# Opening of a retention and two-layer kernel: first half tile of weights loaded second, keys scaled in their own step

## The chip, the cores and the metric

One core of one Trainium2 chip. The metric is the device time of one execution in microseconds (us), as the median of several runs.

## What is computed

Four sequences of 576 tokens, 8 heads of 64 columns, go through a retention layer (attention whose scores are multiplied by a decay in place of a softmax), then through two pairs of dense layers, one with a softplus and one with a sigmoid gate between them:

```python
gamma = 1.0 - 2.0 ** (-5.0 - np.arange(H))
Dmat = np.where(rel >= 0, gamma[:, None, None] ** rel[None, :, :], 0.0)   # rel = i - j
x = ((q @ k.T / 8) * Dmat) @ v            # per batch and head, then 2304 tokens x 512
h = x @ w_in;   x = softplus(h) @ w_out   # w_in 512 x 2048, w_out 2048 x 512
h = x @ w_in2;  out = (h * sigmoid(1.702 * h)) @ w_out2
```

## The kernel before, in words

Every engine has its own queue and works it off in order; the order in which the program issues instructions is the order of these queues, and the framework adds the waits between engines.

**First batch.** `first_batch` (L568) computes the retention of batch 0 before anything else can start. Its work is eight "pairs" i = 0 to 7: two heads by 256 tokens each, of which odd i are the later tokens of the heads of i-1. The loop at L607 runs ten times; iteration i calls `step(i - 2, i, ...)` (L387), which puts the scores and the state sums of pair i and the output of pair i-2 through TensorE (PE). In the order of PE's queue, step i is: scores k by q (L409); for odd i a small product of the last 64 tokens; the state sums, scaled keys by values (L397, `ps<-w_kqv`); then the output of pair i-2 from the known state (`<-w_kqv,w_sv`) and from its masked scores (`<-w_a,w_kqv`). Then ScalarE (ACT) multiplies the scores with the decay of the rows (L436, twice) and, for even i, copies the state sums (L94, `w_sv<-ps_h`); VectorE (DVE) updates the state (L443, called state update below), for odd i masks the last scores (L450), and writes the output xf (L456, and L461 for odd i); GpSimd (POOL) masks the scores (L446). The sums of state and the output of one step lie in one bank of PSUM.

**Scaling of keys.** Before the state sums, the keys of each pair are multiplied with a decay by `scale_pair` (L373): one head on ACT (L385) and one on POOL (L383); for pair 0 both on ACT. `scale_pair(i + 1, "ap", "p")` at L614 issues POOL's half of pair i+1 ahead of step i, `scale_pair(i + 2, "ap", "a")` at L619 ACT's half of pair i+2 behind step i.

**Split for the first layer.** PE multiplies in parts: every operand is split into a rounded high part and the rest. Behind each odd step from 3 on, `split_x` issues ACT's cast xh of two pairs (L94) and, one iteration later, DVE's subtraction xl (L99). One quarter of xh and xl belongs to each pair of heads; the last quarter comes in two halves behind iterations 8 and 9. The first layer (`run_first`, `mm1`, L220; its matmuls are at L211) starts when the loop is over, and needs the four quarters one after the other.

**Weights.** Each weight arrives as a 64-bit word and is turned into high and low part by `convert_first` (L113), a generator of which `next` issues a piece. For one half tile (a unit): `get`, ACT's rescaling (L132); `go`, DVE's L104 and L105; `merge`, DVE's L110; ACT's cast (L94, `w<-wa`); DVE's subtraction (L99, `w<-wa,w`). Units 0 and 1 are the first layer's weights of the first two of 16 blocks, unit 2 those of the third, unit 3 the first of the second layer's. How many pieces follow each iteration stands in the table at L689.

**Loads.** SyncE (SP) issues the loads of the eight pairs (512 KB each), of the decays, of the last tokens ("ends"), and of the weights (512 KB each) in the order of L586 to L602. SP's queue issues a transfer when the eighth before it has landed: while loads are pending, its issue times are landing times.

Of the kernel before, what the change touches and what calls it, by code (L numbers as in the profile page):

```python
# [33 lines left out]
def kernel(  # L34
# [37 lines left out]
    B, _, NPAIR, _, KQV = kqv.shape  # L72
# [19 lines left out]
    def hi(eng, dst, src):  # L92
        if eng == "a":
            nc.scalar.copy(dst, src)  # L94
        else:
            nc.vector.tensor_copy(dst, src)
# [5 lines left out]
    def shift(w, a):  # L102
        u = a.bitcast(U32)
        nc.vector.tensor_single_scalar(out=u, in_=u, scalar=3, op=ALU.logical_shift_left)  # L104
        nc.vector.scalar_tensor_tensor(  # L105
            out=u, in0=w[:, :, 1], scalar=0x80000000, in1=u, op0=ALU.bitwise_and, op1=ALU.bitwise_or)

    def merge(w, a):
        u = a.bitcast(U32)
        nc.vector.scalar_tensor_tensor(  # L110
            out=u, in0=w[:, :, 0], scalar=29, in1=u, op0=ALU.logical_shift_right, op1=ALU.bitwise_or)

    def convert_first(units, slots, raw, tiles, loaded, made):  # L113

        opening, n = 3, len(units)
        held, shifted, room = {}, set(), {}  # L120

        def words(i):
            k, m = units[i][0], len(units[i])
            return raw[k // 2][:, k % 2:k % 2 + m].rearrange("p s n two -> p (s n) two")

        def get(i):
            if i < n and i not in held and all(k in loaded for k in units[i]):
                k, m = units[i][0], len(units[i])
                if k // 2 not in room:
                    room[k // 2] = wr.tile([P, 2, DM], F32, tag="wa", name="wa")  # L130
                a = room[k // 2][:, k % 2:k % 2 + m].rearrange("p s n -> p (s n)")
                nc.scalar.mul(a, words(i)[:, :, 1].bitcast(F32), 2.0 ** -112)  # L132
                held[i] = a

        def go(i):
            shift(words(i), held[i])
            shifted.add(i)

        for i in range(n):
            while i not in held:  # L140
                get(i)
                yield
            if i not in shifted:
                go(i)
                if 0 < i < opening:
                    get(i + 1)
                yield
            merge(words(i), held[i])
            yield
            if i >= opening:  # L150
                get(i + 1)
            k, m = units[i][0], len(units[i])
            if k // 2 not in tiles:
                tiles[k // 2] = wp.tile([P, 2, 2, DM], F32R, tag="w", name="w")
            h, l = (tiles[k // 2][:, k % 2:k % 2 + m, j] for j in range(2))
            a = held[i].rearrange("p (s n) -> p s n", s=m)
            hi("a", h, a)
            if i >= opening and i + 2 < n and len(units[min(i + 1, n - 1)]) == 1:
                get(i + 2)
            yield  # L160
            if i >= opening and i + 1 in held and (m == 2) == (len(units[i - 1]) == 2):
                go(i + 1)
                yield
            lo(l, a, h)
            made.update(slots[k] for k in units[i])
            if i < opening:
                get(i + 1) if i == 0 else None
            yield

    def convert(n, ready, words, place, begin, end):  # L170
# [133 lines left out]
    with tc.manual_schedule():  # L304
# [36 lines left out]
        with ExitStack() as consts, ExitStack() as right, ExitStack() as second:  # L341
            ac = consts.enter_context(tc.tile_pool(name="ac", bufs=1))
            ap = right.enter_context(tc.tile_pool(name="ap", bufs=2, side="right"))
# [29 lines left out]
            def scale_pair(i, engines="aa", only="ap"):  # L373
                p, x = pairs[i][2], loaded[i][2]
                if i >= 2 * NPAIR:
                    nc.scalar.mul(x, x, sdec64[:, p:p + 1])
                    return
                for h in range(2):
                    y, d = x[:, :, halves[h]], sdec[:, 2 * p + h:2 * p + h + 1]
                    if engines[h] not in only:  # L380
                        continue
                    if engines[h] == "p":
                        nc.gpsimd.tensor_scalar(out=y, in0=y, scalar1=d, scalar2=None, op0=ALU.mult)  # L383
                    else:
                        nc.scalar.mul(y, y, d)  # L385
# [182 lines left out]
            def first_batch():  # L568

                n = 2 * NPAIR  # L570
                xf[0] = xf_tile()
                raw = [wp.tile([P, 2, KQV], F32, tag="w", name="w_kqv") for _ in range(NPAIR)]
                end = wp.tile([P, 2, KQV], F32, tag="w", name="w_end")
                end = end.rearrange("p s n -> p (s n)")[:, 0:NPAIR * ENDS].rearrange("p (a n) -> p a n", a=NPAIR)
                sv0 = wp.tile([P, 2, 8, P], F32, tag="w", name="w_sv")
                sv0 = [[sv0[:, i, j, 0:D] for j in range(4)] for i in range(2)]
                a0 = wp.tile([P, 4 * DM], F32, tag="w", name="w_a")
                a0 = [a0[:, i * (2 * C0 + D):(i + 1) * (2 * C0 + D)] for i in range(3)]

                def load(i):  # L580
                    load_pair(i, raw[i // 2][:, i % 2], end[:, i // 2])

                def load_end(p, n):
                    nc.sync.dma_start(out=end[:, p:p + n], in_=ends[0, :, p:p + n])

                load(0)  # L586
                nc.sync.dma_start(out=dec, in_=decays)
                load(1)
                load_end(0, 1)
                load(2)  # L590
                w1_load(0)
                load(3)
                nc.sync.dma_start(out=odec, in_=outdecay)
                load_end(1, 1)
                load(4)
                w1_load(1)
                load(5)
                load_end(2, 2)
                load(6)
                w1_load(2)  # L600
                load(7)
                w1_load(3, 4, 5)  # L602
                scale_pair(0)
                scale_pair(1, "ap", "a")
                yield
                late = []
                for i in range(n + 2):  # L607
                    if i % 2:
                        banks = [bank(ps_y, "y") for _ in range(3)]
                    else:  # L610
                        so = ps_a.tile([P, 2, T], F32, tag="so", name="ps_so")
                        banks = [bank(ps_h, "h"), so[:, 0], so[:, 1]]
                    if i + 1 < n:
                        scale_pair(i + 1, "ap", "p")  # L614
                    while late:
                        late.pop(0)()
                    step(i - 2 if i >= 2 else None, i if i < n else None, banks, sv0, a0)
                    if i + 2 < n:
                        scale_pair(i + 2, "ap", "a")  # L619
                    if i == n:  # L620
                        late.append(split_x(0, 1, xf[0], NPAIR - 1, slice(0, C0)))
                    elif i == n + 1:
                        late.append(split_x(0, 1, xf[0], NPAIR - 1, slice(C0, T)))
                    elif i >= 3 and i % 2:
                        late.append(split_x(0, 1, xf[0], i // 2 - 1))
                    for _ in range(1 if i < FILL else 0):
                        warm()
                    if i == n + 1:
                        while late:
                            late.pop(0)()  # L630
                    yield
# [29 lines left out]
            def w1_load(*ks):  # L661

                for k in ks:
                    if k >= len(slots):
                        continue
                    if k // 2 not in w1_raw:
                        w1_raw[k // 2] = wp.tile([P, 2, DM, 2], U32, tag="w", name="w_raw")
                    f, s = slots[k]
                    nc.sync.dma_start(
                        out=w1_raw[k // 2][:, k % 2].rearrange("p n two -> p (n two)"),  # L670
                        in_=w_src(w1_in, w1_out, f, s))
                    w1_loaded.add(k)
# [12 lines left out]
            for i, _ in enumerate(first_batch()):  # L685
                if i == 9:
                    w1_load(6, 7)
                    nc.sync.dma_start(out=dmask.rearrange("p a d -> p (a d)"), in_=masks)
                for _ in range({5: 2, 7: 2, 8: 2, 9: 2}.get(i, 1) if i >= 2 else 0):  # L689
                    next(w1_gen, None)  # L690


# [696 lines left out]
```

## Time and profile before

| what | value |
|---|---|
| time before, median of 3 runs | 837.8 us (835.58, 837.8, 838.04) |
| the profiled execution's own time | 835.43 us |
| its span, first to last instruction | 833.7 us |
| PE busy | 822.2 us, 99% of the span |
| DVE, ACT, POOL busy | 583.7, 407.6, 99.6 us |
| granted clock of PE, mean | 0.999 of full speed |

A row of the timeline gives the start of an instruction from the span's start, its duration, the engine, the line, the operation, output <- inputs, how many instructions are merged (x2), and in brackets how long the engine stood idle before it and what ended that. The next start on the same engine can lie before the end of an instruction, since they overlap a little in the engine.

### The profile page before, as it was taken

To read this page: it belongs to the slowest core of one execution; us is meant where nothing else is said; L and a number is where in the kernel's file an instruction comes from. 1 tells how busy PE (TensorE), PEld (TensorE's weight loads), DVE (VectorE), ACT (ScalarE), POOL (GpSimd) and SP (SyncE) were. 2 spreads that over 40 slices of the span, in tenths; PEclk is the share of its full clock that TensorE was granted. 3 is DMA by queue.
4 is the path that set the end of the run, shared out by engine and by line. 5 is a ranking of instruction groups with operands and counts; after the bars stand their busy time and mean duration, and the time that the engine had idled before them with its cause. 6 is when DMAs were issued, how large, how long until landed. Compare 5 with 4: busy or idle time off the path is not lost.

```text
span 833.7 us, 17016 instructions
## 1 busy us (share of the span) xinstructions
PE 822.2 (99%) x6810; PEld 742.0 (89%) x6811; DVE 583.7 (70%) x1206; ACT 407.6 (49%) x797; POOL 99.6 (12%) x185
## 2 busy tenths in 40 slices
PE   8899999999999999999999999999999999999998
PEld 6788788888888888998888899999999999999997
DVE  3999996666676664775543667787778777866665
ACT  5666654433443434453434545554555555554332
POOL 3200001111211120001011011211121111111010
PEclk9999999999999999999999999999999999999999
DMA  9966325887787674899996677887799778776691
GB/s 339 407 272 244 119 88 188 274 270 239 236 262 263 231 236 171 303 359 387 418 367 210 227 279 243 314 316 241 260 328 320 242 266 327 280 246 215 234 361 55
DMA packets 63438, 221.71 MB, mean 266 GB/s; under 512 B 6448, under 2 KB 20080, under 8 KB 50304
## 3 DMA queue, kind: packets, MB, share of 16 engines
q0 software_dynamic: 21600, 122.76, 42.4%
q1 hardware_dynamic: 41440, 97.62, 32.1%
q8 instruction: 53, 0.87, 0.4%
q10 hardware_dynamic: 320, 0.26, 0.1%
q14 instruction: 25, 0.20, 0.1%
HBM read 163.99 MB, written 56.62 MB: 265 GB/s over the span
## 4 chain that ended last, share of the span: by engine, by line
PE 79%; issue 8%; DVE 7%; DMA 3%; ACT 1%; POOL 1%; SPq 0%; POOLq 0%; ACTq 0%
PE y L211 22%; PE ph L211 22%; PE ph L893 17%; PE m L893 16%; PE ps_so L477 3%; DMA xo<-x 1%; DMA w_kqv<-kqv 1%; POOL w L812 1%; DVE wa L110 1%; DVE wa L105 1%; DMA w_end<-ends 1%; DVE wa L104 1%; DVE w L99 0%; DVE ga L99 0%; DVE sv L529 0%
## 5 line engine op out<-in xcount | busy, mean ns | idle before, releaser
L211 PE MATMUL ph<-xh,w 128*128 128x512 f32 (+1 forms) x640 | 183.4, 371 | 0.9 <-ACT xh L94 0.6
L211 PE MATMUL y<-gh,w 128*128 128x512 f32 x512 | 169.9, 392 | 0.0
L893 PE MATMUL m<-w,ga 128*128 128x256 f32 x936 | 139.5, 282 | 0.1
L211 PEld LDWEIGHTS ph<-xh,w 128*128 128x128 f32 x640 | 114.8, 188 | 22.5 <-ACT xh L94 1.0
L893 PEld LDWEIGHTS m<-w,ga 128*128 128x128 f32 x936 | 124.0, 190 | 0.3 <-DVE ga L99 0.3
L211 PE MATMUL ph<-xl,w 128*128 128x512 f32 (+1 forms) x320 | 117.9, 368 | 0.0
L211 PEld LDWEIGHTS y<-gh,w 128*128 128x128 f32 x512 | 95.9, 188 | 20.1
L893 PE MATMUL ph<-xo_c,w 128*128 128x256 f32 x768 | 108.2, 283 | 0.8 <-DVE he L1140 0.8
L893 PE MATMUL ph<-xo,w 128*128 128x256 f32 x768 | 105.8, 283 | 1.4 <-DVE ho L1180 0.8
L893 PEld LDWEIGHTS ph<-xo,w 128*128 128x128 f32 x768 | 97.7, 189 | 3.0 <-DVE ho L1180 1.9
L893 PEld LDWEIGHTS ph<-xo_c,w 128*128 128x128 f32 x768 | 97.8, 188 | 2.2 <-DVE he L1140 1.4
L211 PE MATMUL y<-gl,w 128*128 128x512 f32 x256 | 99.8, 390 | 0.0
L265 ACT ACTIVATE g<-ph 128x512 f32<-128x512 f32 (+1 forms) x80 | 44.1, 552 | 96.4 <-PE ph L211 90.7
L893 PE MATMUL m<-w,gb 128*128 128x256 f32 x576 | 89.7, 282 | 0.0
L99 DVE TENSOR_TENSOR gl<-g,gh 128x512 fp32r<-128x512 f32 x64 | 44.0, 688 | 54.9 <-ACT gh L94 54.6
L893 PEld LDWEIGHTS m<-w,gb 128*128 128x128 f32 x576 | 78.0, 191 | 0.0
L211 PEld LDWEIGHTS ph<-xl,w 128*128 128x128 f32 x320 | 60.2, 188 | 10.2 <-DVE xl L99 0.2
L99 DVE TENSOR_TENSOR gb<-g,gb 128x256 fp32r<-128x256 f32 x112 | 43.9, 420 | 24.8 <-ACT gb L94 24.7
L94 ACT CAST ga<-g 128x512 fp32r<-128x512 f32 x80 | 49.6, 621 | 15.9 <-DVE g L745 6.5
L211 PEld LDWEIGHTS y<-gl,w 128*128 128x128 f32 x256 | 48.1, 188 | 9.5
L99 DVE TENSOR_TENSOR ga<-g,ga 128x512 fp32r<-128x512 f32 x80 | 52.6, 685 | 0.4 <-ACT ga L94 0.2
L104 DVE TENSOR_SCALAR wa<-wa 128x512 uint32<-128x512 uint32 (+1 forms) x53 | 25.9, 488 | 32.3 <-ACT wa L179 32.3
(147 smaller groups left out, 1119.0 us busy)
## 6 DMA issues: line engine op xcount, KB each, us to landing
w<-sums_out POOLq DMA_DIRECT2D x40, 1024.0 KB, 7.9
w<-sums_in POOLq DMA_DIRECT2D x32, 1024.0 KB, 5.3
raw<-kqv SPq DMA_DIRECT2D x24, 512.0 KB, 5.3
w<-kept POOLq DMA_DIRECT2D x12, 1024.0 KB, 8.9
w_raw<-w_in SPq DMA_DIRECT2D x16, 512.0 KB, 9.3
w_raw<-w_out SPq DMA_DIRECT2D x16, 512.0 KB, 9.9
raw<-w_in POOLq DMA_DIRECT2D x16, 512.0 KB, 5.8
raw<-w_out POOLq DMA_DIRECT2D x16, 512.0 KB, 5.7
```

The source lines that it names most:

```text
L94: nc.scalar.copy(dst, src)
L99: nc.vector.tensor_tensor(out=dst, in0=src, in1=f32(h), op=ALU.subtract)
L104: nc.vector.tensor_single_scalar(out=u, in_=u, scalar=3, op=ALU.logical_shift_left)
L105: nc.vector.scalar_tensor_tensor(out=u, in0=w[:, :, 1], scalar=0x80000000, in1=u, op0=ALU.bitwise_and, op1=ALU.bitwise_or)
L110: nc.vector.scalar_tensor_tensor(out=u, in0=w[:, :, 0], scalar=29, in1=u, op0=ALU.logical_shift_right, op1=ALU.bitwise_or)
L211: nc.tensor.matmul(out_ap, l, r, start=first and i == 0, stop=last and i == k - 1)
L265: nc.scalar.activation(g, ph, AF.Softplus)
L477: nc.tensor.matmul(z[halves[m], o, at:at + D], l[halves[g]], rhs[halves[g]], start=clear[o][m], stop=True, skip_group_check=True)
L812: nc.gpsimd.dma_start(out=where[i], in_=src)
L893: nc.tensor.matmul(out_ap, l, r, start=clear, stop=True, skip_group_check=True)
```

## The change

The first half tile of weights is loaded right behind pair 0 and the decays, and the second ahead of pair 4; the conversion starts behind iteration 0 and gets another number of pieces per iteration (table at L689); the rescaling `get` of units 1 and 2 is issued at another piece; and both halves of the keys' scaling of pair i are issued at the head of iteration i.

```diff
@@ convert_first
             if i not in shifted:
                 go(i)
-                if 0 < i < opening:
+                if i == opening - 1:
                     get(i + 1)
                 yield
...
             made.update(slots[k] for k in units[i])
-            if i < opening:
-                get(i + 1) if i == 0 else None
             yield
@@ first_batch
                 load(0)
                 nc.sync.dma_start(out=dec, in_=decays)
+                w1_load(0)
                 load(1)
                 load_end(0, 1)
                 load(2)
-                w1_load(0)
                 load(3)
+                load_end(1, 1)
                 nc.sync.dma_start(out=odec, in_=outdecay)
-                load_end(1, 1)
+                w1_load(1)
                 load(4)
-                w1_load(1)
                 load(5)
...
                 scale_pair(0)
-                scale_pair(1, "ap", "a")
                 yield
...
-                    if i + 1 < n:
-                        scale_pair(i + 1, "ap", "p")
+                    if 0 < i < n:
+                        scale_pair(i, "ap")
                     while late:
                         late.pop(0)()
                     step(i - 2 if i >= 2 else None, i if i < n else None, banks, sv0, a0)
-                    if i + 2 < n:
-                        scale_pair(i + 2, "ap", "a")
@@ behind the loop's iterations
-                for _ in range({5: 2, 7: 2, 8: 2, 9: 2}.get(i, 1) if i >= 2 else 0):
+                for _ in range({2: 2, 3: 2, 7: 3, 10: 2}.get(i, 1) if i else 0):
                     next(w1_gen, None)
```

Lines behind L145 move up by up to five: the scaling on ACT is L385 before and L383 in the change, the scores' decay L436 and L434, the state update L443 and L441, the output xf L456 and L454.

**ACT, steps 3 to 5, before.** The scores of pair 3 (L436), then the scaling of pair 5 (L385), the cast xh of the first quarter, step 4, the scaling of pair 6, the conversion's cast and rescaling, and the scores of pair 5:

```order
L436 ACTIVATE w_a<-ps_y,dec 128x256 x2
L385 ACTIVATE w_kqv<-w_kqv,dec 128x2x64
L94 CAST xh<-xf 128x512
L436 ACTIVATE w_a<-ps_so,dec 128x256 x2
L94 COPY w_sv<-ps_h 128x64
L385 ACTIVATE w_kqv<-w_kqv,dec 128x2x64
L94 CAST w<-wa 128x512
L132 ACTIVATE wa<-w_raw 128x512
L436 ACTIVATE w_a<-ps_y,dec 128x256 x2
```

The same place in the change, from the scores of pair 3 to those of pair 5:

```order
L434 ACTIVATE w_a<-ps_y,dec 128x256 x2
L94 CAST xh<-xf 128x512
L132 ACTIVATE wa<-w_raw 128x512
L383 ACTIVATE w_kqv<-w_kqv,dec 128x2x64
L434 ACTIVATE w_a<-ps_so,dec 128x256 x2
L94 COPY w_sv<-ps_h 128x64
L383 ACTIVATE w_kqv<-w_kqv,dec 128x2x64
L434 ACTIVATE w_a<-ps_y,dec 128x256 x2
```

The two scalings here are those of pairs 4 and 5, each directly ahead of the scores of its own pair; the cast xh and the rescaling of unit 1 stand ahead of the first.

**ACT, steps 6 and 7, in the change**, from the cast xh behind step 5 to the scores of pair 7:

```order
L94 CAST xh<-xf 128x512
L383 ACTIVATE w_kqv<-w_kqv,dec 128x2x64
L434 ACTIVATE w_a<-ps_so,dec 128x256 x2
L94 COPY w_sv<-ps_h 128x64
L94 CAST w<-wa 128x512
L132 ACTIVATE wa<-w_raw 128x512
L383 ACTIVATE w_kqv<-w_kqv,dec 128x2x64
L434 ACTIVATE w_a<-ps_y,dec 128x256 x2
```

Before, the scaling of pair 7 stood ahead of this xh and the rescaling of unit 2 ahead of the scores of pair 6; now the copy of step 6, the cast of unit 1 and the rescaling of unit 2 stand ahead of the scaling of pair 7.

**DVE, steps 6 and 7, before**, with the waits that each instruction carries (numbers aside, the names are engines and DMA queues): the state update and xf of step 6, unit 1's L110, the state update, end mask and xf of step 7, and the last subtraction of unit 1:

```order
L443 SCALAR_TENSOR_TENSOR w_sv<-w_sv,dec,ps_h 128x64 [waits Activation_49]
L456 TENSOR_TENSOR xf<-ps_h,odec 128x256
L110 SCALAR_TENSOR_TENSOR wa<-w_raw,wa 128x512 [waits DVE_49]
L443 SCALAR_TENSOR_TENSOR w_sv<-w_sv,dec,ps_y 128x64 [waits DVE_49,PE_49]
L443 SCALAR_TENSOR_TENSOR w_sv<-w_sv,dec,ps_y 128x64 [waits DVE_49]
L450 SCALAR_TENSOR_TENSOR w_a<-ps_y,dec,mask 128x64
L456 TENSOR_TENSOR xf<-ps_y,odec 128x256
L461 TENSOR_TENSOR xt<-ps_y,odec 128x64
L99 TENSOR_TENSOR w<-wa,w 128x512 [waits Activation_49]
```

The same place in the change:

```order
L441 SCALAR_TENSOR_TENSOR w_sv<-w_sv,dec,ps_h 128x64 [waits Activation_49]
L454 TENSOR_TENSOR xf<-ps_h,odec 128x256
L99 TENSOR_TENSOR w<-wa,w 128x512 [waits Activation_49]
L441 SCALAR_TENSOR_TENSOR w_sv<-w_sv,dec,ps_y 128x64 [waits DVE_49,PE_49]
L441 SCALAR_TENSOR_TENSOR w_sv<-w_sv,dec,ps_y 128x64 [waits DVE_49]
L448 SCALAR_TENSOR_TENSOR w_a<-ps_y,dec,mask 128x64
L454 TENSOR_TENSOR xf<-ps_y,odec 128x256
L459 TENSOR_TENSOR xt<-ps_y,odec 128x64
```

Unit 1's L110 has gone further up and its L99 has moved from behind step 7's group to ahead of it. In both, the row that writes xf from the out matmuls carries no wait of its own for PE; the state update ahead of it does (odd steps), or ACT's copy that it waits for (even steps).

## Rows read from the trace of the kernel before

**Rows 1.** Stretches: span, busy time (instructions) by engine, granted clock, DMA share, GB/s.

```profile
25.00:30.00 5.00, 3.84 (x40) 3.16 (x41) 4.93 (x13) 2.91 (x7) 2.49 (x4) 1.00 1.03 403
30.00:35.00 5.00, 4.39 (x19) 3.22 (x19) 4.56 (x11) 3.86 (x8) 0.00 (x0) 1.00 1.03 412
35.00:80.00 45.00, 45.00 (x403) 37.14 (x403) 43.19 (x72) 29.16 (x43) 0.00 (x0) 1.00 0.75 286
...
400.00:800.00 400.00, 397.82 (x3071) 385.13 (x3070) 278.92 (x579) 199.16 (x426) 49.39 (x93) 1.00 0.78 279
```

**Rows 2.** Timeline of ACT: scalings of pairs 1, 4, 5 and 7.

```profile
7.06 0.40 ACT L385 ACTIVATE w_kqv<-w_kqv,dec 128x128 f32<-128x128 f32 x1 [1.67 <-DMA w_kqv<-kqv]
...
13.70 0.40 ACT L385 ACTIVATE w_kqv<-w_kqv,dec 128x128 f32<-128x128 f32 x1 [0.59 <-DMA w_kqv<-kqv]
...
16.28 0.40 ACT L385 ACTIVATE w_kqv<-w_kqv,dec 128x128 f32<-128x128 f32 x1 [1.45 <-DMA w_kqv<-kqv]
...
21.52 0.40 ACT L385 ACTIVATE w_kqv<-w_kqv,dec 128x128 f32<-128x128 f32 x1 [0.34 <-DMA w_kqv<-kqv]
```

**Rows 3.** Timeline of PE: step 2, and step 5 from its state sums on.

```profile
8.87 0.71 PE L409 MATMUL ps_so<-w_kqv 64*128 64x128 f32 x8 [0.23 <-DMA w_kqv<-kqv]
9.52 0.47 PE L397 MATMUL ps_h<-w_kqv 128*64 128x64 f32 x8
...
10.28 0.66 PE L397 MATMUL ps_h<-w_a,w_kqv 128*64 128x128 f32 x8
...
17.33 0.43 PE L397 MATMUL ps_y<-w_kqv 128*64 128x64 f32 x8
...
18.87 0.28 PE L397 MATMUL ps_y<-w_a,w_end 128*64 128x64 f32 x4
```

**Rows 4.** Timeline of POOL: scaling of half of pair 2, mask of pair 1.

```profile
8.88 0.60 POOL L383 TENSOR_SCALAR w_kqv<-w_kqv,dec 128x128 f32<-128x128 f32 x1
...
9.96 0.64 POOL L446 TENSOR_SCALAR_AFFINE_SELECT w_a<-w_a 128x512 f32<-128x512 f32 x1 [0.47 <-ACT w_a L436]
```

**Rows 5.** Timeline of ACT: cast xh, rescaling, scores and copy of step 6, cast, scores of step 7.

```profile
21.83 0.60 ACT L94 CAST xh<-xf 128x512 fp32r<-128x512 f32 x1
...
22.34 0.69 ACT L132 ACTIVATE wa<-w_raw 128x512 f32<-128x512 f32 x1
...
22.92 0.83 ACT L436 ACTIVATE w_a<-ps_so,dec 128x256 f32<-128x256 f32 x2
...
23.64 0.21 ACT L94 COPY w_sv<-ps_h 128x64 f32<-128x64 f32 x1
...
25.13 0.62 ACT L94 CAST w<-wa 128x512 fp32r<-128x512 f32 x1 [1.28 <-DVE wa L110]
...
25.65 0.83 ACT L436 ACTIVATE w_a<-ps_y,dec 128x256 f32<-128x256 f32 x2
```

**Rows 6.** Timeline from pair 7's state update to the first layer's last quarter.

```profile
25.01 0.59 DVE L443 SCALAR_TENSOR_TENSOR w_sv<-w_sv,dec,ps_y 128x64 f32<-128x64 f32 x2
...
25.71 0.41 DVE L456 TENSOR_TENSOR xf<-ps_y,odec 128x256 f32<-128x256 f32 x1
...
26.18 0.68 DVE L99 TENSOR_TENSOR w<-wa,w 128x512 fp32r<-128x512 f32 x1
...
26.77 0.86 DVE L104 TENSOR_SCALAR wa<-wa 128x512 uint32<-128x512 uint32 x1
...
27.41 0.66 PE L397 MATMUL ps_y<-w_a,w_kqv 128*64 128x128 f32 x8 [1.16 <-POOL w_a L446]
27.67 0.69 DVE L105 SCALAR_TENSOR_TENSOR wa<-w_raw,wa 128x512 uint32<-128x512 uint32 x1
...
28.11 0.73 PE L211 MATMUL ph<-xh,w 128*128 128x512 f32 x2
...
30.60 0.40 ACT L94 CAST xh<-xf 128x256 fp32r<-128x256 f32 x1
31.05 0.73 PE L211 MATMUL ph<-xh,w 128*128 128x512 f32 x2 [0.61 <-ACT xh L94]
```

## The prediction

> **What bounds the kernel now.** I read the stretch table first, to see which engine each stage waits on. From 35 us to 80 TensorE (PE) is busy for 45.00 of 45.00 us, and from 400 to 800 for 397.82 of 400.00; only before 35 us does it stand still for a whole microsecond and more (3.84 of 5.00 at 25 to 30, 4.39 at 30 to 35) [rows 1]. So PE sets the time, and an edit of the opening is worth exactly what it moves one instant: the first matmul of the first layer on the last quarter of the tokens, at 31.05 us, which waits 0.61 for ScalarE's (ACT's) xh [rows 6]. Behind it PE does not stop until 80, so a later start is not made up, and VectorE (DVE), busy for 43.19 of those 45 us [rows 1], has nothing to spare for an earlier one either.
>
> I then followed that instant backwards in the timeline. Two clocks run through the opening. One is the landing of the head pairs: pair 1 at 7.06, pair 4 at 13.70, pair 5 at 16.28, pair 7 at 21.52, read from the scalings that waited for them [rows 2]; 5.24 us for the two steps from pair 5 to pair 7, one 512 KB transfer each 1.29 (13.70 to 16.28 holds two). The other is each step's chain over the engines. Today the keys of pair i+2 are scaled at the end of step i on ACT and those of i+1 at the start of step i on GpSimd (POOL), so PE finds them scaled soon after landing and the steps keep the pace of the landings. Behind the last landing the tail is a DVE queue: the state update of pair 7 starts at 25.01 and 6.04 us later, at 31.05, PE has its input [rows 6].
>
> **The change, part by part.**
>
> *Loads.* The first half tile of weights goes ahead of pair 1, so pairs 1 and 2 land one transfer later, 1.29; pair 4 too, since the second half tile goes ahead of it. Pairs 3, 5, 6 and 7 keep their place: pair 7 is the sixteenth issue of SyncE's queue both before and after. The last landing stays at 21.52, so this edit alone costs 0 to 1.3 and is swallowed by what follows. The two small transfers that swap places (decays of the output, ends of pair 1) are needed only after pair 3 has landed: nothing.
>
> *Conversion.* The same DVE operations for half tiles 0 and 1 are queued earlier; from the first operation of half tile 2 on, DVE's queue is the same row for row. The only one that leaves the tail is the last operation of half tile 1 (L99, 26.18 to 26.77, 0.59) [rows 6]; before, it lay between pair 7's state update and the end. Gain in the tail 0.6, and up to 1.0 if L104 behind it, which took 0.90 beside POOL's mask (26.77 to 27.67), no longer meets one; I take 0.8: 5.2 from pair 7's state update to PE's input.
>
> *Scaling.* This decides. ACT is one in-order queue, and the scaling of pair i now stands in it behind everything that step i-1 left there: its copy of the state sums, and its casts. PE's queue is in order as well: the state matmuls of step i wait for the scaling, and the out matmuls of pair i-2 stand behind them. So a loop closes that was open. The rows of waits show what makes it long: L454, which reads the out matmuls, carries no wait for PE, so L441 ahead of it must already have waited for all matmuls of that bank, the out matmuls included; for even steps the same goes for ACT's copy. I take these waits as they stand. No row of the trace can show them bind, as DVE and ACT were always later; the other bound is rival 2. The Trainium skill, "PSUM — Partial Sum Buffer", section "PSUM bank collisions raise a hardware error", says that two engines must not touch one bank in the same partitions at once and that schedulers therefore order such pairs; by it the sum below stands, without it rival 2 does, and no row of this trace decides.
>
> The loop from the end of an odd step's out matmuls to the next one's:
> - 0.1 handover; DVE state update, end mask and xf 1.11 (25.01 to 26.12); ACT cast xh 0.51 (21.83 to 22.34); scaling 0.40 and handover 0.05; PE state, state-out and out matmuls of the even step 1.42 (9.52 to 10.94); ACT copy 0.21 and handover; then the scaling of the odd pair 0.45; PE of the odd step from its state matmuls to its last 1.82 (17.33 to 19.15) [rows 2, 3, 5, 6]. Together 6.1.
> - From step 3 to 5, L132 of half tile 1 stands between cast and scaling, 0.58 (22.34 to 22.92): 6.7. From step 5 to 7, the cast of half tile 1, 0.52 (25.13 to 25.65), and L132 of half tile 2, 0.58, stand ahead of the scaling of pair 7 [rows 5]: 7.2.
>
> Against 5.24 for two steps of landings, so from step 3 on the landings no longer matter. Start of the count: pair 1 lands at 8.35 (7.06 + 1.29); scores 0.71, ACT's two scalings of them 0.83, POOL's mask 0.64 and, behind it in POOL's queue now, the scaling of half of pair 2, 0.60, with handovers 11.3; step 2 on PE 1.42, copy 0.2, the cast of half tile 0 that now stands there 0.52, scaling of pair 3 0.45: 13.9; step 3 on PE 1.82, handover 0.1: state update of pair 3 at 15.8 [rows 2 to 5]. Pair 5's follows at 22.5, pair 7's at 29.7; it was at 25.01. Plus 5.2: PE's input is ready at 34.9 to 35.2 in place of 31.05. **Sum: +3.9 to +4.2; I take +4.1 us.** The gaps of PE that show it: about 2.2 ahead of step 4's state matmuls, 1.6 ahead of step 6's, 1.2 ahead of step 7's; the wait of 1.16 for POOL's mask at 27.41 [rows 6] goes.
>
> The profiled execution took 835.43, which gives 839.5; the median of the runs is 837.8, which gives 841.9. Two of the four times shown stand near 835.5 and two near 837.9, so I count from their mean, 836.7: **841 us**, +0.5%. A measurement of this kernel tells about 0.3%, 2.5 us, from no change.
>
> **Rivals.**
> 1. *The forecast*, the loop through ACT's queue: 839.5 to 842. For it: each wait of the loop stands in the order rows, and each duration in a row. Against it: the sum of some fifteen handovers that I could only estimate. Chance 0.57.
> 2. *The loop is shorter*, because reads of a bank do not wait for the out matmuls. Then state update and end mask (0.70) leave the path in the three odd steps, 2.1, and the copy of an even step leaves 0.95 earlier, of which 0.2 stays in step 2, nothing in step 4 (POOL's mask and scaling, 0.64 + 0.60, take its place) and 0.8 in step 6: 3.1 less, so +1.0: 837.7. Against it: L454's missing wait. Chance 0.18.
> 3. *No effect*: the tail behind the last landing sets the end, and it only swaps one DVE operation for another delay: 836 to 837.5. For it: 21.52 stays. It needs the steps to catch up with the landings, so a loop under 5.24. Chance 0.09.
> 4. *Faster*: the casts no longer wait in ACT behind a landing, pair 7's mask comes early, and the tail loses its stalls. The most that this can give: from 21.6, scores and end 0.8, state and out matmuls of steps 7 to 9 some 4.1, then the nine matmuls of the first three quarters, 2.3 (28.11 to 30.44, where the wait of 0.61 begins) [rows 6], reach 28.8, which is 2.2 before 31.05: 834.5. It decides only if each loop stays under 5.24. Chance 0.06.
> 5. *Clock*. The granted clock is 1.00 in every stretch of the opening [rows 1], with PE gaps of 1.2 at most; the forecast's gaps are up to 2.2, three in a row. If it fell to 1.2 GHz for these steps, the PE parts of the loops, 2 x (1.42 + 1.82) and 3.2 ahead of them, would double: up to +9.7 more, 844 to 851. The Trainium skill, "TensorE: Matmul & The Clock Gate", section "A second HAM failure mode: psum-queue depth-cycling", tells of a PE that idles briefly and often between groups and swings between the two levels; by that rule this would happen here, while the trace, which has such gaps at 1.00, so far bears the opposite out. Chance 0.10.
>
> **How the numbers follow.** Slower by over 0.3%: 0.50 of case 1, all of 5 and 0.02 of 2, 0.62 in all. Within 0.3%: 0.07 of 1, 0.16 of 2, 0.08 of 3 and 0.02 of 4, so 0.33. Faster by over 0.3%: the rest of 3 and 4, 0.05. The range reaches from case 2 counted from the fast executions (835.5 + 1.0, 836.5) to case 1 counted from the slow ones with handovers 0.2 longer at a dozen places (837.9 + 4.1 + 2.4, 844.4); below lie case 4 and half of 3, above most of 5, together under 0.2.
>
> **What would show it.** Right: the scalings (now L383) start long after their landing, pair 7's near 27.5 in place of 21.52; PE waits for ACT ahead of the state matmuls of steps 4, 6 and 7; pair 7's state update near 30; first matmul of the last quarter near 35; from there the same distances as before. Wrong: scalings of pairs 5 to 7 still released by a DMA (3 or 4), state updates that start before the out matmuls of their step have ended (2), a granted clock below 1.00 before 35 us (5), or PE standing still less after 35 us than before.

## The result, and the profile after

| what | before | change |
|---|---|---|
| median, 6 runs each | 836.24 us (835.45 to 838.04) | 843.93 us (840.45 to 847.29) |
| ratio | 1 | 1.0086, 95% interval 1.0056 to 1.0115 |
| the profiled execution: own time, span | 835.43, 833.7 us | 844.08, 842.3 us |
| its granted clock, mean | 0.999 | 0.994 |

The change costs 7.7 us. First the stretches of the changed kernel, with the columns of [rows 1]: span, busy time (instructions) of PE, PE's weight loads, DVE, ACT and POOL, granted clock, DMA share, GB/s.

```profile
5.00:10.00 5.00, 2.14 (x20) 1.61 (x21) 0.28 (x1) 2.29 (x7) 0.87 (x2) 0.91 0.96 353
10.00:15.00 5.00, 5.00 (x45) 3.55 (x45) 2.48 (x6) 1.98 (x6) 2.48 (x5) 0.50 1.03 413
15.00:20.00 5.00, 3.95 (x60) 3.13 (x57) 2.42 (x8) 1.96 (x6) 1.78 (x3) 0.90 1.03 407
20.00:25.00 5.00, 3.56 (x42) 2.81 (x44) 2.34 (x6) 3.46 (x9) 1.22 (x2) 0.78 1.02 409
25.00:30.00 5.00, 3.46 (x48) 2.85 (x48) 2.46 (x7) 1.65 (x4) 1.37 (x3) 0.88 1.03 406
30.00:35.00 5.00, 4.22 (x66) 3.24 (x64) 2.13 (x7) 2.31 (x6) 3.12 (x6) 1.00 1.03 407
...
400.00:800.00 400.00, 397.80 (x3038) 383.80 (x3037) 275.29 (x573) 199.35 (x427) 47.59 (x90) 1.00 0.79 284
```

The kernel before in the same stretches, up to where [rows 1] begin:

```profile
5.00:10.00 5.00, 4.77 (x57) 3.55 (x58) 1.04 (x4) 2.76 (x9) 1.87 (x4) 1.00 0.98 358
10.00:15.00 5.00, 4.12 (x64) 3.39 (x65) 1.82 (x5) 2.92 (x8) 2.67 (x5) 1.00 1.03 412
15.00:20.00 5.00, 4.94 (x84) 3.96 (x80) 3.00 (x10) 2.79 (x8) 2.60 (x4) 1.00 1.03 406
20.00:25.00 5.00, 4.48 (x70) 3.40 (x66) 4.65 (x12) 3.50 (x9) 2.02 (x3) 1.00 1.03 409
```

From 400 to 800 PE is as busy as in [rows 1]: 397.80 against 397.82 us. The opening differs twice. From 5 to 35 PE stands still for 7.67 of 30 us where before it stood still for 3.46; and the clock, 1.00 throughout before, falls to 0.50, the level of 1.2 GHz, from 10 to 15 and again for parts of 20 to 30. What PE waited for in the changed kernel, in total, times and longest:

```profile
PE ps_h L395 <- ACT w_kqv L383: 3.6, 2, 2.1
PE ps_y L407 <- DMA w_kqv<-kqv: 2.9, 1, 2.9
...
PE ps_y L395 <- ACT w_kqv L383: 0.8, 1, 0.8
```

Three waits for ACT's scaling (L383), as forecast, and one of 2.9 for a landing. Where they stand, in the timeline, shows the whole path to the last quarter:

```profile
9.61 0.40 ACT L383 ACTIVATE w_kqv<-w_kqv,dec 128x128 f32<-128x128 f32 x1 [0.64 <-DMA w_kqv<-kqv]
9.63 1.22 PE L407 MATMUL ps_y<-w_kqv 64*128 64x128 f32 x8 [2.86 <-DMA w_kqv<-kqv]
...
14.57 1.12 PE L395 MATMUL ps_h<-w_a,w_kqv 128*64 128x128 f32 x8
...
15.73 0.21 ACT L94 COPY w_sv<-ps_h 128x64 f32<-128x64 f32 x1 [1.46 <-PE ps_h L395]
...
18.42 0.28 PE L395 MATMUL ps_y<-w_a,w_end 128*64 128x64 f32 x4
...
18.75 0.60 DVE L441 SCALAR_TENSOR_TENSOR w_sv<-w_sv,dec,ps_y 128x64 f32<-128x64 f32 x2 [1.56 <-PE ps_y L395]
...
19.91 0.62 ACT L94 CAST xh<-xf 128x512 fp32r<-128x512 f32 x1 [2.17 <-DVE xf L454]
20.43 0.67 ACT L132 ACTIVATE wa<-w_raw 128x512 f32<-128x512 f32 x1
...
21.00 0.39 ACT L383 ACTIVATE w_kqv<-w_kqv,dec 128x128 f32<-128x128 f32 x1
...
21.44 0.45 PE L395 MATMUL ps_h<-w_kqv 128*64 128x64 f32 x8 [2.09 <-ACT w_kqv L383]
...
22.78 1.23 PE L407 MATMUL ps_y<-w_kqv 64*128 64x128 f32 x8
...
26.92 0.60 DVE L441 SCALAR_TENSOR_TENSOR w_sv<-w_sv,dec,ps_y 128x64 f32<-128x64 f32 x2 [2.10 <-PE ps_y L395]
...
29.05 0.45 PE L395 MATMUL ps_h<-w_kqv 128*64 128x64 f32 x8 [1.54 <-ACT w_kqv L383]
...
31.70 0.39 ACT L383 ACTIVATE w_kqv<-w_kqv,dec 128x128 f32<-128x128 f32 x1
...
32.14 0.45 PE L395 MATMUL ps_y<-w_kqv 128*64 128x64 f32 x8 [0.78 <-ACT w_kqv L383]
...
34.04 0.60 DVE L441 SCALAR_TENSOR_TENSOR w_sv<-w_sv,dec,ps_y 128x64 f32<-128x64 f32 x2 [2.08 <-PE ps_y L395]
...
39.05 0.74 PE L209 MATMUL ph<-xh,w 128*128 128x512 f32 x2 [0.42 <-ACT xh L94]
```

One turn of the loop can be read off from 18.75 to 26.92: state update of pair 3, xh at 19.91 behind its xf, the rescaling at 20.43, only then the scaling of pair 4 at 21.00, PE's state matmuls at 21.44 after 2.09 of standing still. The last row stood at 31.05 [rows 6]: 8.00 of the 8.65 us between the two profiled executions lie ahead of it, and 0.60 behind it (842.3 - 39.05 against 833.7 - 31.05). Two rows say that the clock was low: the scores of a pair took 1.22 and 1.23 us (9.63, 22.78) where [rows 3] have 0.71.

### The profile page after: what moved, and what is told of

The parts are those of the page before. It is cut to its first block, busy times and chain, and to the rows that moved or that the text cites. A ratio compares the mean times of both kernels' runs of the same rounds, so it can differ in the third digit from the quotient of the medians.

```text
span 842.3 us, 17016 instructions
## 1 busy us (share of the span) xinstructions
PE 826.0 (98%) x6810; PEld 744.3 (88%) x6811; DVE 583.2 (69%) x1206; ACT 407.1 (48%) x797; POOL 98.6 (12%) x185
## 4 chain that ended last, share of the span: by engine, by line
PE 74%; DVE 9%; issue 9%; DMA 5%; ACT 2%; POOL 1%; SPq 0%; POOLq 0%; DVEq 0%; ACTq 0%
PE y L209 18%; PE ph L209 18%; PE ph L888 17%; PE m L888 16%; PE ps_so L475 3%; DMA sums_in<-sum_halves 1%; DVE wa L105 1%; DVE wa L110 1%; DMA xo<-x_t 1%; PE ps_y L395 1%; DMA w_kqv<-kqv 1%; POOL w L807 1%; DVE wa L104 1%; DMA sums_out<-sum_halves 1%; DVE w L99 1%
## 5 line engine op out<-in xcount | busy, mean ns | idle before, releaser
L99 DVE TENSOR_TENSOR gl<-g,gh 128x512 fp32r<-128x512 f32 x64 | 44.1, 689 | 63.6 <-ACT gh L94 63.6
L99 DVE TENSOR_TENSOR gb<-g,gb 128x256 fp32r<-128x256 f32 x112 | 43.9, 420 | 25.5 <-ACT gb L94 25.5
L99 DVE TENSOR_TENSOR ga<-g,ga 128x512 fp32r<-128x512 f32 x80 | 52.6, 686 | 0.7 <-ACT ga L94 0.4
L94 ACT CAST gb<-g 128x256 fp32r<-128x256 f32 x112 | 45.4, 407 | 0.8
```

Of the source, the lines that this page charges most:

```text
L99: nc.vector.tensor_tensor(out=dst, in0=src, in1=f32(h), op=ALU.subtract)
```

## The experiments

The **loop** theory: ACT's scaling behind the casts of the step before closes the loop of the prediction. Its rivals: **landing**, the weights ahead of pair 1 cost by themselves; **clock**, the time beyond the loop is the granted clock and not more waiting. The kernel before was run beside all of them, 836.24 and 836.18 us.

**1. Scaling back ahead, the rest of the change kept.**

```diff
+                scale_pair(1, "ap", "a")
...
-                    if 0 < i < n:
-                        scale_pair(i, "ap")
+                    if i + 1 < n:
+                        scale_pair(i + 1, "ap", "p")
...
+                    if i + 2 < n:
+                        scale_pair(i + 2, "ap", "a")
```

> The change's loads and conversion, with the scaling of keys ahead as before. Loop theory (the scaling's place in ACT's queue costs some 4 us): the last quarter's first matmul returns from 39.05 to between 30.5 and 32.5, and the time to 835.5 to 838. Clock and landing theory (the late landing of pair 1 and the low clock behind it cost most of the 8 us): it stays at 34 or later, 839 to 841.

Measured: 836.32 us, 1.0002 [0.9985, 1.0019]; in the profile pair 1 landed at 9.31 and the last quarter began at 32.92. Loads and conversion of the change together move the time by nothing that can be measured, so its loss hangs on the scaling. The last quarter began 0.4 later than the loop theory's range allows (30.5 to 32.5), and the clock was low in this profile too (0.58 from 10 to 15, 0.74 from 15 to 20), at 836.99 us: a low clock behind the landing doesn't by itself make the loss.

**2. The scaling alone, in the kernel before** (the same edit, the other way round).

```diff
-                scale_pair(1, "ap", "a")
...
-                    if i + 1 < n:
-                        scale_pair(i + 1, "ap", "p")
+                    if 0 < i < n:
+                        scale_pair(i, "ap")
...
-                    if i + 2 < n:
-                        scale_pair(i + 2, "ap", "a")
```

> The kernel before, with only the scaling moved into its own step. Loop theory: pair 5's and pair 7's state updates lie 6.7 to 7.3 apart while the granted clock is 1.00, and the time is 839.5 to 842. Clock and landing theory: pair 1 lands at 7.06 as before, the clock stays at 1.00 at least to 16 us, and the time is 836 to 838.

Measured: 844.74 us, 1.0087 [1.0056, 1.0117]: the whole loss, with pair 1 landed at 7.50. The state updates of pairs 3, 5 and 7 in its timeline, and the first matmul of the last quarter:

```profile
17.24 0.60 DVE L443 SCALAR_TENSOR_TENSOR w_sv<-w_sv,dec,ps_y 128x64 f32<-128x64 f32 x2 [1.67 <-PE ps_y L397]
...
24.37 0.59 DVE L443 SCALAR_TENSOR_TENSOR w_sv<-w_sv,dec,ps_y 128x64 f32<-128x64 f32 x2 [2.09 <-PE ps_y L397]
...
34.27 0.60 DVE L443 SCALAR_TENSOR_TENSOR w_sv<-w_sv,dec,ps_y 128x64 f32<-128x64 f32 x2 [4.28 <-PE ps_y L397]
...
39.88 0.74 PE L211 MATMUL ph<-xh,w 128*128 128x512 f32 x2 [0.31 <-ACT xh L94]
```

Its stretches around them:

```profile
15.00:20.00 5.00, 3.47 (x60) 2.73 (x56) 3.03 (x8) 2.44 (x6) 1.22 (x2) 0.97 1.03 406
20.00:25.00 5.00, 4.18 (x64) 3.24 (x60) 1.81 (x6) 2.37 (x7) 2.44 (x4) 1.00 1.03 410
...
30.00:35.00 5.00, 4.00 (x38) 3.32 (x40) 0.70 (x4) 1.65 (x4) 2.37 (x4) 0.50 1.03 410
```

From pair 3 to 5 at a clock of 0.97 to 1.00 the loop takes 7.13; from 5 to 7, where the clock falls to 0.50, 9.90. Not all of the 2.77 more is clock: ACT's cast ahead of pair 7's scaling waited 1.28 for DVE's L110, which the conversion of the change issues earlier (there the cast starts without a wait, at 30.61):

```profile
30.02 0.62 ACT L94 CAST w<-wa 128x512 fp32r<-128x512 f32 x1 [1.28 <-DVE wa L110]
```

The loop stands, the later landing isn't needed for the loss, and the clock falls without it. The median lies above the ranges of both theories; the one execution at a mean clock of 0.999 took 840.58, within that of the loop. That the loss is as large as the change's is in part chance: pair 1 lands 2.1 earlier here, and the wait of 1.28 and the longer tail of before are added.

**3. The order of the loads alone, in the kernel before.**

```diff
                 nc.sync.dma_start(out=dec, in_=decays)
+                w1_load(0)
                 load(1)
...
-                w1_load(0)
                 load(3)
-                nc.sync.dma_start(out=odec, in_=outdecay)
                 load_end(1, 1)
-                load(4)
+                nc.sync.dma_start(out=odec, in_=outdecay)
                 w1_load(1)
+                load(4)
```

> The kernel before, with only the order of its loads changed. Landing theory: the first half tile lands at 8.3, pair 1 at 9.6, pair 7 at 22.7, PE waits 2.5 us or more for pair 1 and the granted clock falls to 0.5 there; 837 to 840. If the later landings were chance: pair 1 at 8.35, pair 7 at 21.5, 836 to 837.5. Loop theory alone: no more than 1.3 us over before.

Measured: 839.13 us, 1.0018 [0.9999, 1.0037]. Its median lies 2.9 us above, its interval just touches no change, and its ten executions reach from 835.17 (mean clock 1.000) to 840.39 (0.994). The profiled one lost clock; pair 1's scores, and the stretch behind them:

```profile
9.62 1.22 PE L409 MATMUL ps_y<-w_kqv 64*128 64x128 f32 x8 [3.33 <-DMA w_kqv<-kqv]
```
```profile
10.00:15.00 5.00, 5.00 (x45) 3.55 (x45) 1.03 (x4) 3.63 (x11) 3.44 (x6) 0.50 1.04 413
```

So the executions of the new order that lose clock take up to some 4 us more, and the one that keeps it (835.17) nothing; beside the new conversion (experiment 1) the order's cost doesn't show in the median. Whether the order alone costs anything stays open by these runs. The kernel before loses clock now and then as well: of its 24 executions beside this one, three took 839.34 to 840.05, at mean clocks of 0.997 and 0.998.

**4. The change with PE kept busy.** More of the program's own warm-up matmuls, whose result nothing reads, stand in PE's queue where it would wait: ten behind step 0, and eight, six and three between the scores and the state sums of steps 4, 6 and 7.

```diff
-                    for _ in range(1 if i < FILL else 0):
+                    for _ in range({0: 11}.get(i, 1) if i < FILL else 0):
                         warm()
...
                             nc.tensor.matmul(ps[h][:, j], k[r, j], q[r, j], start=True, stop=True)
+                    for _ in range({4: 8, 6: 6, 7: 3}.get(i, 0)):
+                        warm()
```

> The change, with 10 more warm matmuls ahead of step 1 and 8, 6 and 3 of them between scores and state sums of steps 4, 6 and 7, in gaps in which PE stood idle. Loop and clock together: granted clock 1.00 from 5 to 35 us, last quarter's first matmul at 35.5 to 37 in place of 39.05, 839.5 to 841.5 in every execution. Loop alone without the clock: no change from 843.9. Clock alone without the loop: 835.5 to 837.5.

Measured: 840.17 us (839.34 to 841.54), 1.0042 [1.0029, 1.0055], clock 1.00 in every stretch. The same four rows as in experiment 2:

```profile
16.87 0.60 DVE L443 SCALAR_TENSOR_TENSOR w_sv<-w_sv,dec,ps_y 128x64 f32<-128x64 f32 x2 [1.52 <-PE ps_y L395]
...
23.56 0.59 DVE L443 SCALAR_TENSOR_TENSOR w_sv<-w_sv,dec,ps_y 128x64 f32<-128x64 f32 x2 [0.62 <-PE ps_y L395]
...
30.69 0.59 DVE L443 SCALAR_TENSOR_TENSOR w_sv<-w_sv,dec,ps_y 128x64 f32<-128x64 f32 x2 [2.09 <-PE ps_y L395]
...
35.70 0.73 PE L209 MATMUL ph<-xh,w 128*128 128x512 f32 x2 [0.43 <-ACT xh L94]
```

6.69, 7.13 and 5.01: the three terms of the prediction (6.7, 7.2, 5.2), at full clock. The added matmuls ended before the scalings that PE waited for, so they delayed none of its work in steps 4, 6 and 7. The loop by itself, with the start that the loads give it, costs 3.9 us (840.17 against 836.24); the other 3.8 of the change go with the clock. The change's own executions agree: the two with mean clocks of 1.000 and 0.998 took 841.09 and 840.45. The added matmuls make PE do more and the kernel faster, which no theory of waiting alone gives.

**5. ACT's half one step ahead and ahead of the casts, POOL's in its own step.**

```diff
-                        scale_pair(i, "ap")
+                        scale_pair(i, "ap", "p")
...
+                    if i + 1 < n:
+                        scale_pair(i + 1, "ap", "a")
```

> The change, with ACT's half of the scaling of pair i+1 issued right behind step i and ahead of the casts; POOL's half stays in its own step. If only the casts ahead of ACT's half cost: the last quarter's first matmul at 32 to 33, 836.5 to 838. If POOL's half has its own loop: 33.5 to 36, 838.5 to 841.5.

Measured: 839.76 us, 1.0055 [1.0033, 1.0078], last quarter at 34.02. PE waits in steps 5 and 7 for POOL's half, and once still for ACT's:

```profile
20.07 0.33 PE L395 MATMUL ps_y<-w_kqv 128*64 128x64 f32 x2 [0.69 <-ACT w_kqv L383]
21.22 0.45 PE L395 MATMUL ps_y<-w_kqv 128*64 128x64 f32 x6 [0.82 <-POOL w_kqv L381]
...
27.03 0.45 PE L395 MATMUL ps_y<-w_kqv 128*64 128x64 f32 x6 [0.61 <-POOL w_kqv L381]
```

The state updates lie 6.58 and 5.80 apart (16.54, 23.12, 28.92) at a clock of 1.00, both above the 5.24 of the landings; with ACT's half behind the casts, at the same clock, it was 6.69 and 7.13 (experiment 4). So the casts ahead of ACT's half account for 1.4 of the 3.3 us by which the two turns exceed the landings, and POOL's half keeps a loop going. Most of the 4.2 us gained on the change can be clock: experiment 4, which left the scaling as it was, gained 3.8.

**6. The conversion alone:** the loads and the scaling of before, with the change's conversion. Against before it differs only in this:

```diff
-                if 0 < i < opening:
+                if i == opening - 1:
                     get(i + 1)
...
-            if i < opening:
-                get(i + 1) if i == 0 else None
...
-                for _ in range({5: 2, 7: 2, 8: 2, 9: 2}.get(i, 1) if i >= 2 else 0):
+                for _ in range({2: 2, 3: 2, 7: 3, 10: 2}.get(i, 1) if i else 0):
```

> The kernel before, with the change's conversion steps alone: loads in their order before and scaling ahead. If what the change gives back in the tail (one DVE operation less behind pair 7's state update) counts when nothing else is delayed: last quarter's first matmul at 29.5 to 30.8, granted clock 1.00, 834.5 to 836, faster than both kernels by 0.3 to 1.5. If DVE's queue only shifts its wait: 836 to 837.

Measured: 835.22 us (834.51 to 837.0, 11 executions), 0.999 [0.998, 1.000]. From its pair 7's state update to the last quarter:

```profile
24.50 0.59 DVE L441 SCALAR_TENSOR_TENSOR w_sv<-w_sv,dec,ps_y 128x64 f32<-128x64 f32 x2
...
25.66 0.54 DVE L104 TENSOR_SCALAR wa<-wa 128x512 uint32<-128x512 uint32 x1
...
29.62 0.73 PE L209 MATMUL ph<-xh,w 128*128 128x512 f32 x2 [0.59 <-ACT xh L94]
```

5.12 in place of 6.04 [rows 6]: L99 has left the tail, and L104 takes 0.54 in place of 0.86. This is the one part of the change that may be worth having, and the lowest median of all: 1.0 us below before, at the edge of what can be told from no change. The profiled execution itself shows no gain: it starts the last quarter 1.43 earlier than before and yet spans 833.9 against 833.7 us. What lies behind that instant took 802.65 us before and 804.28 here, and between 802.38 and 804.28 in the ten profiles read for this document; an instant of the opening gives the time of a single execution to within some 2 us, not exactly.

**7. Only ACT's half in its own step, in the kernel before.**

```diff
-                scale_pair(1, "ap", "a")
...
+                    if 0 < i < n:
+                        scale_pair(i, "ap", "a")
                     if i + 1 < n:
                         scale_pair(i + 1, "ap", "p")
...
-                    if i + 2 < n:
-                        scale_pair(i + 2, "ap", "a")
```

> The kernel before, with only ACT's half of the scaling in its own step, POOL's half still ahead. If ACT's queue alone closes the loop: PE waits for ACT ahead of the state matmuls of steps 4 and 6, pair 5's and pair 7's state updates lie 7 or more apart at full clock (4.5 before), and the time is 840 to 845, as with both halves moved. If it is POOL's half: PE waits of under 0.5 there and 836 to 837.5.

Measured: 845.24 us, 1.0115 [1.0101, 1.0128], last quarter at 41.44. What PE waited for:

```profile
PE ps_h L397 <- ACT w_kqv L385: 4.7, 3, 1.7
...
PE ps_y L397 <- ACT w_kqv L385: 1.1, 1, 1.1
```

ACT's half alone gives a loss as large as the change's, and again the clock lies between 0.50 and 0.84 from 10 to 35. So the 8.96 and 9.88 between its state updates (16.99, 25.95, 35.83) are no measure of the loop at full clock, for which 7 was expected; as in experiment 2, the cast ahead of pair 7's scaling also waited 1.28 for DVE's L110.

**8. Only POOL's half in its own step, in the kernel before.**

```diff
-                    if i + 1 < n:
-                        scale_pair(i + 1, "ap", "p")
+                    if 0 < i < n:
+                        scale_pair(i, "ap", "p")
```

> The kernel before, with only POOL's half in its own step, ACT's half still two ahead. Rival to the ACT loop: POOL's queue is in order too, and the half then stands behind the mask of the step before, which waits for ACT's scores, so that this alone closes a loop of its own: 838 to 842, with PE waiting for POOL ahead of the state matmuls. ACT's queue alone: 836 to 837.5.

Measured: 841.49 us, 1.0068 [1.0054, 1.0082], last quarter at 36.02. The place in step 7, with ACT's cast in front of it:

```profile
23.41 0.62 ACT L94 CAST xh<-xf 128x512 fp32r<-128x512 f32 x1 [1.89 <-DVE xf L456]
...
25.45 0.64 POOL L446 TENSOR_SCALAR_AFFINE_SELECT w_a<-w_a 128x512 f32<-128x512 f32 x1 [2.94 <-ACT w_sv L94]
26.07 1.08 POOL L383 TENSOR_SCALAR w_kqv<-w_kqv,dec 128x128 f32<-128x128 f32 x1
...
27.20 0.64 PE L397 MATMUL ps_y<-w_kqv 128*64 128x64 f32 x6 [1.99 <-POOL w_kqv L383]
```

POOL's half closes a loop too: the mask of pair 6, which needs the scores that ACT has scaled, stands ahead of the scaling of pair 7, and PE waits 1.99 for it. This loop runs through ACT as well, since those scores stand behind the cast xh, which waits for the step before. The clock fell here too (0.73 from 25 to 30), but one execution at a mean clock of 1.000 took 841.46, so most of this loss isn't clock. The two losses don't add (845.24 and 841.49 apart, 844.74 together), since both delay the same state matmuls.

## Why the prediction came out as it did

The forecast was slower by 4.1, 841.0 us in a range of 836.5 to 844.4; measured were 843.93 and +7.7. The mechanism was right, the size about half. That 843.93 still lies in the range is in part luck: the upper end was made of handovers 0.2 longer at a dozen places, counted from the higher of the times before (837.9), and what took the time to 843.93 was the start of the count and the clock.

**Confirmed: the loop.** PE waits for ACT ahead of the state matmuls of steps 4, 6 and 7, by 2.09, 1.54 and 0.78 (forecast 2.2, 1.6 and 1.2), the wait for POOL's mask is gone, and pair 7's scaling starts at 31.70, nine microseconds after its landing (the transfer that waits for it in SyncE's queue is issued at 22.73). The terms "pair 5 to 7" and "tail" are met in the change itself: 7.12 and 5.01 against 7.2 and 5.2.

**Refuted: the shorter loop.** ACT's copy at 15.73 starts when the out matmuls of its bank (14.57, 1.12 long) have ended, not when the state sums ahead of them have, and has stood idle 1.46 for them; the state update at 18.75 follows the last out matmul (18.42 + 0.28). Both read columns of the bank that those out matmuls don't write. The rule of the Trainium skill, "PSUM — Partial Sum Buffer", section "PSUM bank collisions raise a hardware error", by which schedulers order two engines that touch one bank in the same partitions, agrees with these two waits; whether the framework waits for the sake of the bank or because one tile fills it, no run here separates.

**Mis-sized: the start of the count.** Forecast for pair 3's state update was 15.8, measured 18.75. Two terms make this.
- "Pairs 1 and 2 land one transfer later, 1.29" was too small: pair 1 landed at 9.61 and not at 8.35, 1.26 later still. Over the profiled executions it landed at 7.06, 7.50, 6.34, 7.20 and 5.92 with the old order (mean 6.8) and at 9.61, 9.31, 9.60, 9.33 and 8.67 with the new (mean 9.3), 2.5 later. "The last landing stays at 21.52" was off as well, by 1.2 (22.73), without effect, since nothing waited for it any more.
- The clock: from that landing to the update it took 9.14, where the forecast has 7.45 (15.8 - 8.35) and experiment 4, at full clock, 7.54 (16.87 - 9.33). That is 1.6 more.

**Wrongly weighed: the clock as a rival with a chance of 0.10.** It was priced as something that happens instead of the forecast, and it happens along with it. The falls go with the wait of 2.86 for pair 1 (ended at 9.63, at a clock already low), and with the wait of 2.09 ahead of step 4's state matmuls, which the forecast itself had named (ended at 21.44, with the low clock from 22.78 on). The second fall makes the turn from pair 3 to 5 8.17 in place of 6.69. So 1.6 + 1.5 = 3.1 us of the profiled execution are clock, and the rest of the miss ahead of the last quarter, 39.05 - 34.9 - 3.1 = 1.05, is the late landing (1.26) less what the last two terms came out shorter (0.08 and 0.19), to within 0.06. The argument against, that the trace of before had gaps at 1.00, rested on gaps of 1.2 at most and didn't reach to those of 2 and 3. The rule of the Trainium skill that was named for that rival ("TensorE: Matmul & The Clock Gate", section "A second HAM failure mode: psum-queue depth-cycling", swings between the levels where PE idles briefly and often) agrees in part: the clock does swing, with 0.50, 0.90, 0.78, 0.88 and 1.00 in succession, but in this profile each fall goes with one wait of over 2 us, and the waits of 1.54 and 0.78 passed without a fall. The weight given to it was too small.

**Missed: POOL's half.** The prediction counted POOL's scaling as 0.60 behind the mask of step 1 and let ACT decide from there. Experiment 8 shows that moving it costs 5.3 us alone; in the change the rows of waits name ACT alone, whose half comes later and hides it.

**Right: conversion.** The tail was to gain 0.8; experiment 6 measures 0.92.

**Open: the loads alone.** They were priced at 0 to 1.3. Experiment 3 has a median 2.9 above, with an interval that touches no change, and experiment 1 no difference; in the change they act through the start of the count, by more than assumed.

**Too strict: the first premise.** An edit of the opening was to be worth "exactly" what it moves the last quarter's first matmul. In the change 8.00 of the 8.60 us between the spans lie ahead of that instant, but experiment 6 moved it by 1.43 and its profiled span by nothing.

**Left open:** why the landing moved by two transfers' time where one was put ahead of it. One half of it can be placed: SyncE's queue shows the third transfer landed at 7.05 before, where it is pair 1, and at 8.31 in the change, where it is the half tile (means of five profiles each: 6.8 and 8.0), and pair 1 followed 1.3 behind the half tile. Open as well is why executions of one kernel lose the clock to different degrees: six executions of the change run from 840.45 (mean clock 0.998) to 847.29 (0.990).

## What to carry over

In a pipeline over in-order queues, work on an operand that depends on a load alone should be issued ahead of everything on its engine that depends on the step before; put behind that, it ties the steps into a loop whose length replaces the pace of the loads, and each engine that does a part of it closes one. Compute such a loop as a sum and compare it with that pace; where the sum predicts gaps of PE longer than any that the trace shows at full clock, price the clock into the forecast rather than beside it. To tell a gap's own cost from the clock's, fill the gaps with matmuls that nothing reads: in experiment 4 the loop kept its length and the clock stayed at 1.00.

## What was not expected of the hardware

Half a megabyte put ahead of another transfer delayed that by 2.5 us (five executions each way) where a transfer takes 1.29 in the steady stream. And two waits, of 2.86 for pair 1 and 2.09 for the scaling of pair 4, went with falls of the clock that cost nearly as much again, 3.8 us of medians, as the loop itself, 3.9.
